# Two PSUM banks in one Relu instruction, and buffers that are cut by hand, in a fused attention and maxout kernel

## The chip, the core and the metric

The kernel runs on one core of a Trainium2 chip. The metric is the device time of one execution in microseconds (us); lower is better. The engines that appear below are TensorE (PE, matmuls; its weight loads are listed as PEld), VectorE (DVE), ScalarE (ACT), GpSimd (POOL) and SyncE (SP, which issues most DMAs). PSUM is the memory that PE writes its results to; it has 8 banks, and one bank holds 512 float32 numbers on each of 128 partitions.

## What is computed

Cut to what matters, with B = 4 batches of N = 12544 rows, C = 128 channels, 32 inducing points and J = 1024 hidden columns:

```python
def mab(q, kv):
    a = softmax(scale * q @ kv.T)
    return a @ kv
h = mab(inducing, x)              # 32 x 128 for each batch
y = mab(x, h)                     # 12544 x 128 for each batch
out = maximum(y @ w1, y @ w2) @ w_out
```

The kernel uses maximum(p, q) = p + relu(q - p). The part relu(y @ (w2 - w1)) @ w_out is the bulk of the work; y @ w1 @ w_out is one small matrix product, called the linear part.

## The kernel before

For each batch the rows are handled in chunks of 128 rows (98 chunks a batch). Up to 16 chunks make a block of four quarters, and a quarter holds up to four chunks. `stage` (L643) writes exp(scale * h x^T) of a block to SBUF, with the quarter q on the partitions 32q to 32q+31. Division by the sum of the exponentials is put off until the output.

A **phase** (L1031) takes up to four units, one for each quarter. A unit is 512 columns of hidden values: one to four matmuls with a contraction of 32 (L1085), which use only a quarter of PE's rows, so that four units run side by side. Each unit fills one PSUM bank. After the phase, each bank is **evicted**: Relu from PSUM to an SBUF tile in float16, by ACT (L1102) or DVE (L1105), whichever the planner thinks is free first. `final_one` (L920) then issues one full matmul (L932) that multiplies 128 hidden columns of a chunk by w_out and adds to the bank of the running **group** (a group is a quarter's chunks, up to four, in one bank that stays open for up to 32 such matmuls and a few of the linear part). `evict_group` (L954) divides by the sums, writes the result to SBUF and stores it with a DMA.

The order is written out by hand. `ORDER` (L1113) is a list of words: `p4.5` is a phase of four units whose bits in 5 swap the engine that the planner would choose, a number is that many final matmuls, `s` stages a block, `g3` transposes a block's exponentials with a DMA for POOL to sum, `x1.0` transposes x of the next batch, and so on. `Clock` (L21) is a planner: it adds up estimated durations to choose banks and engines while the program is built, and it is not run on the chip. All waits between engines are put in by the framework, which compares what each instruction reads and writes.

Before the steady part there is a ramp of some 27 us. Batch 0 of x is loaded by POOL's DMAs in twelve parts (`load_x`, L190, L195); each part is transposed (L276), multiplied by the inducing points (L292), put through exp (L305), and accumulated (L328) together with the sums of the exponentials (E sums, L319: up to four chunks of 32 columns by one matmul with a column of ones). Then come h, its product with w2 - w1 (`difference`, L572, and `small_hwd`, L506), and the weight work for the linear part: `cast_w1` (L576), `weights_2` (transposes, L589), `weights_2b` (L593) and `weights_3` (L603, eight matmuls at L607). `keep_busy` (L879) adds filler matmuls where the planner sees a gap.

PSUM tiles, Relu tiles and output tiles come from pools: a tile has a name of its own, and the framework knows which earlier tile held its place.

## Time and profile before

| what | value |
|---|---|
| median of 3 runs | 317.82 us (317.73 to 318.14) |
| profiled execution, its own time | 317.76 us |
| span of the profile (first to last instruction) | 316.0 us |
| PE busy | 308.6 us, 98% |
| ACT busy | 280.2 us, 89% |
| DVE busy | 274.5 us, 87% |
| POOL busy | 125.8 us, 40% |
| granted TensorE clock, mean | 0.998 |
| instructions | 12577 |

A busy share counts the time in which at least one instruction of the engine was running. In a group of instructions, the mean is of one instruction from its start to its end; since an engine starts the next one before the last has ended, a run of n takes less than n means. The chain of waits is followed back from the last instruction, and tells which engine's work set the end.

### The profile page before, as it was taken

Reading aid. Unit: us, or ns where it says so; the run is one execution under the profiler, and the core shown is the slowest. Engines: PE = TensorE matmul, PEld = TensorE weight load, DVE = VectorE, ACT = ScalarE, POOL = GpSimd, SP = SyncE. Lnnn points to the kernel's source line nnn. Section 1 sums busy time; section 2 is a strip of 40 time slices with the busy share of each in tenths; the row PEclk is TensorE's granted clock in tenths of the full one; section 3 lists DMA queues with packets and bytes.
Section 4 is the critical chain, followed back from the end, with each engine's and each line's share of the span. In section 5 each row is a group of like instructions: output and inputs, shape, how many; then the busy total and the mean of one; then the engine's idle time right before and its main releaser. Section 6 shows DMA issues by size and latency. Waiting matters only on the chain.

```text
span 316.0 us, 12577 instructions
## 1 busy us (share of the span) xinstructions
PE 308.6 (98%) x5308; PEld 239.9 (76%) x5308; DVE 274.5 (87%) x488; ACT 280.2 (89%) x580; POOL 125.8 (40%) x187
## 2 busy tenths in 40 slices
PE   6998999999999999999999999999999999999996
PEld 3885777777877777778877787887868777788885
DVE  2468999999878999988999899989899889999885
ACT  3669999999999999998999989899999999998891
POOL 7363060666620066067510064674406564461500
PEclk9999999999999999999999999999999999999999
DMA  8999999989799999898499999897323233324232
GB/s 203 208 252 205 207 219 146 207 229 230 127 218 245 245 183 174 190 233 207 121 225 252 213 227 215 204 174 203 106 85 118 100 106 118 119 88 140 102 120 101
DMA packets 81336, 55.81 MB, mean 177 GB/s; under 512 B 62816, under 2 KB 66176, under 8 KB 81280
## 3 DMA queue, kind: packets, MB, share of 16 engines
q1 hardware_dynamic: 75312, 41.32, 55.8%
q0 software_dynamic: 5968, 13.70, 22.4%
q8 instruction: 41, 0.67, 0.9%
q14 instruction: 15, 0.12, 0.1%
HBM read 27.28 MB, written 25.69 MB: 168 GB/s over the span
## 4 chain that ended last, share of the span: by engine, by line
PE 94%; DMA 2%; ACT 1%; DVE 1%; issue 1%; POOL 0%; POOLq 0%
PE ps L932 60%; PE ps L1085 23%; DMA xn<-in_x_dram 2%; PE ps L657 2%; PE ps L356 2%; PE ps L414 2%; PE ps L276 1%; PE ps L328 1%; PE ps L292 1%; PE ps L521 0%; DVE relu L1105 0%; PE ps L319 0%; ACT e L669 0%; DVE o L964 0%; ACT e_first L696 0%
## 5 line engine op out<-in xcount | busy, mean ns | idle before, releaser
L1102 ACT ACTIVATE relu<-ps 128x512 f16<-128x512 f32 x470 | 241.0, 627 | 17.5 <-PE ps L1085 16.5
L1105 DVE TENSOR_SCALAR relu<-ps 128x512 f16<-128x512 f32 x314 | 199.7, 684 | 20.6 <-PE ps L1085 19.0
L932 PE MATMUL ps<-woutp,relu 128*128 128x128 f16 x3136 | 203.5, 219 | 0.2
L932 PEld LDWEIGHTS <-relu 128*128 128x128 f16 x3136 | 176.6, 98 | 34.4 <-issue 28.7
L1085 PE MATMUL ps<-e,hwd 32*128 32x512 f16 (+2 forms) x840 | 82.8, 361 | 0.1
L720 POOL TENSOR_TENSOR half<-ed 128x256 f32<-128x256 f16 (+2 forms) x23 | 14.1, 613 | 145.8 <-DMA ed<-e 145.8
L724 POOL TENSOR_TENSOR rd<-den,minus 128x16 f32<-128x16 f32 (+2 forms) x23 | 60.7, 2639 | 1.8
L964 DVE TENSOR_TENSOR o<-ps,rd 128x512 f32<-128x512 f32 (+3 forms) x83 | 53.2, 643 | 3.9 <-PE ps L1085 2.8
L1085 PE MATMUL ps<-m,e 32*128 32x128 f16 x372 | 36.8, 216 | 0.0
L1085 PEld LDWEIGHTS <-hwd 32*128 32x128 f16 x880 | 26.7, 91 | 12.8 <-issue 3.8
L1085 PEld LDWEIGHTS <-e 32*128 32x128 f16 x372 | 22.4, 92 | 10.4 <-issue 2.7
L720 POOL TENSOR_TENSOR half<-half 128x32 f32<-128x32 f32 (+3 forms) x69 | 22.3, 323 | 5.4
L195 POOL DMA_DIRECT2D xn<-in_x_dram x32 | 17.6, 563 | 5.7 <-DMA xn<-in_x_dram 4.3
L280 DVE COPY xT<-ps 128x512 f16<-128x512 f16 (+3 forms) x12 | 5.7, 485 | 8.6 <-PE ps L276 8.6
L964 DVE TENSOR_TENSOR o<-ps,rp 128x512 f32<-128x512 f32 (+3 forms) x20 | 12.8, 642 | 0.0
L369 ACT ACTIVATE eu<-ps 128x512 f16<-128x512 f32 x18 | 11.0, 617 | 0.6 <-PE ps L356 0.3
L669 ACT ACTIVATE e<-ps 128x512 f16<-128x512 f32 (+2 forms) x21 | 11.1, 607 | 0.3 <-PE ps L657 0.2
L283 ACT COPY xT<-ps 128x768 f16<-128x768 f16 (+3 forms) x10 | 5.7, 574 | 4.3 <-PE ps L276 4.2
L276 PE MATMUL ps<-identity,xn 128*128 128x128 f16 x98 | 7.6, 220 | 1.4 <-DMA xn<-in_x_dram 0.9
L657 PE MATMUL ps<-xT,hT 128*32 128x512 f16 (+3 forms) x110 | 8.1, 361 | 0.1
L276 PEld LDWEIGHTS <-xn 128*128 128x128 f16 x98 | 5.5, 97 | 2.9 <-DMA xn<-in_x_dram 1.2
L356 PE MATMUL ps<-xT,inducingT 128*32 128x512 f16 x72 | 6.8, 386 | 0.0
(110 smaller groups left out, 117.7 us busy)
## 6 DMA issues: line engine op xcount, KB each, us to landing
out_dram<-o SPq DMA_DIRECT2D x90, 256.0 KB, 3.0
xn<-in_x_dram POOLq DMA_DIRECT2D x24, 448.0 KB, 10.4
out_dram<-o SPq DMA_DIRECT2D x10, 128.0 KB, 2.9
wf<-in_moe_w_dram POOLq DMA_DIRECT2D x4, 256.0 KB, 6.0
xn<-in_x_dram POOLq DMA_DIRECT2D x4, 224.0 KB, 10.2
xT<-xn SPq DMA_TRANSPOSE x33, 4.4
xf<-in_x_dram SPq DMA_DIRECT2D x1, 512.0 KB, 3.7
xf<-in_x_dram SPq DMA_DIRECT2D x1, 384.0 KB, 4.2
```

Of the source, the lines that this page charges most:

```text
L195: nc.gpsimd.dma_start(out=xn_at[b, i][:, 0:n, :], in_=xr[b, :, k0 : k0 + n, :])
L276: nc.tensor.transpose(ps[:, j, :], xn[:, g + j, :], identity16)
L356: nc.tensor.matmul(out=ps[32 * g : 32 * (g + 1), :], lhsT=inducingT, rhs=xT_tiles[b % 2][:, U * u + 4 * g : U * u + 4 * (g + 1), :], start ...
L657: nc.tensor.matmul(out=ps[32 * q : 32 * (q + 1), 128 * t : 128 * (t + n)], lhsT=hq, rhs=xT[:, c : c + n, :], start=True, stop=True, tile_p ...
L669: nc.scalar.activation(out=blk.e2[:, 0 : 128 * wd], in_=ps[:, 0 : 128 * wd], func=AF.Exp, scale=st[0]["rs"] if blk.b == 0 else scale,)
L720: nc.gpsimd.tensor_tensor(out=dst, in0=cur[:, :, 0:n], in1=cur[:, :, n : 2 * n], op=ALU.add)
L724: nc.gpsimd.tensor_tensor(out=rp[:, 0:wd, :].rearrange("p t q -> p (t q)"), in0=den[:, 0 : 4 * wd], in1=minus1[:, 0 : 4 * wd], op=ALU.pow,)
L932: nc.tensor.matmul(out=g.ps[:, 128 * c : 128 * (c + 1)], lhsT=g.blk.relu[g.q][:, 128 * (jb * w4 + t) : 128 * (jb * w4 + t + 1)], rhs=woutp ...
L964: nc.vector.tensor_mul(osb[:, 0:m, :], g.ps[:, 0 : m * C].rearrange("p (s c) -> p s c", s=m), g.blk.rp[:, t0 : t0 + m, q : q + 1].broadcas ...
L1085: nc.tensor.matmul(**seq.pop(0))
L1102: nc.scalar.activation(out=dst, in_=src, func=AF.Relu)
L1105: nc.vector.tensor_scalar(out=dst, in0=src, scalar1=0.0, scalar2=None, op0=ALU.max)
```

## The change

1. One persistent tensor `psall` [128, 8, 512] takes the place of the PSUM tiles; `bank()` gives slices of it. Four tensors `relus0` to `relus3` with two halves each, two small `relu1_` and one `osbs` with six slots take the place of the pools for Relu and output tiles.
2. `ORDER` has words with a third number (`p4.5.14`): its bits tell which quarters hold their unit back. The next phase of that quarter then evicts both banks with one instruction (`relu_out`, L1050 to L1076 of the new file), with 1024 columns from two banks, a step of b - a banks apart. `u` flushes what is held.
3. E sums take 4 and 3 (or 3 and 3) chunks instead of 4 and 2, and the last two parts of two chunks each share one matmul, so that none has 64 rows of output.
4. In the ramp, one half of `difference` and the second half of `cast_w1` go to POOL, `weights_2` is one step at a later place (`V`), and `weights_3` (`W`) comes later still. The loads of batch 1 are issued around them.
5. Part (0, 7) of x is loaded as 120 and 8 partitions. Seven small DMAs of 15 to 1 partitions copy a few values of part (0, 3) to an unused corner (`probe`).
6. `ORDER` and `EVICT` are new. Some of the planner's numbers are new.

```diff
-    relup = ctx.enter_context(tc.tile_pool(name="relup", bufs=2))
-    outp = ctx.enter_context(tc.tile_pool(name="outp", bufs=NOUT))
...
+    psall = psum.tile([128, 8, 512], F32, name="psall", tag="psall")
+    relus = [big.tile([128, 2, 4096], F16, name=f"relus{q}", tag=f"relus{q}") for q in range(4)]
+    relu1 = [big.tile([128, 1024], F16, name=f"relu1_{q}", tag=f"relu1_{q}") for q in range(2)]
+    osbs = big.tile([128, NOUT, 4, C], F32, name="osbs", tag="osbs")
...
-        uid[0] += 1
-        return i, psum.tile(shape, dtype, name=f"ps{uid[0]}", tag=f"bank{i}", bufs=1)
+        ps = psall[:, i, :]
...
+        return i, ps
...
-        nc.gpsimd.dma_start(out=xn_at[b, i][:, 0:n, :], in_=xr[b, :, k0 : k0 + n, :])
+        cuts = (0, 120, 128) if (b, i) == (0, 7) else (0, 128)
+        for lo, hi in zip(cuts, cuts[1:]):
+            nc.gpsimd.dma_start(out=xn_at[b, i][lo:hi, 0:n, :], in_=xr[b, lo:hi, k0 : k0 + n, :])
...
+        for i, k in enumerate((15, 14, 12, 8, 4, 2, 1)):
+            nc.sync.dma_start(out=probe[0:k, 16 * i : 16 * i + 8 + i], in_=xn_at[0, 3][0:k, 0, 0 : 8 + i])
...
+        SUMS = {
+            14: ((0, 4), (4, 4), (8, 3), (11, 3)),
+            7: ((0, 4), (4, 3)),
+            6: ((0, 3), (3, 3)),
+            4: ((0, 4),),
+        }
+        pair16 = head16[:, 1024 : 1024 + 4 * M].rearrange("p (k m) -> p k m", m=M)
...
-                for j in range(lo, hi, 4):
-                    m = min(4, hi - j)
+                if n > 2:
+                    cuts = [(et, j, m) for j, m in SUMS[n]]
+                else:
+                    cuts = [(pair16, 0, 4)] if last else []
+                for src, j, m in cuts:
...
-                nc.scalar.copy(out=w1h[:, sl], in_=w1f[:, sl])
-                w_of["cast", h] = ck.on_act(21.7, 0.45)
+                nc.gpsimd.tensor_copy(out=w1h[:, sl], in_=w1f[:, sl])
+                w_of["cast"] = ck.on_pool(0.0, 0.8)
...
-        for i in range(7):
-            if i == 3:
-                difference(nc.gpsimd, 512, J, 22.4, 1.2)
+        load_x(1, 0)
+        difference(nc.vector, 0, 256, 21.0, 0.34)
+        difference(nc.gpsimd, 256, 512, 21.0, 0.64)
+        load_x(1, 1)
+        load_x(1, 2)
+        difference(nc.gpsimd, 512, J, 22.9, 1.25)
+        cast_w1(1)
+        for i in range(3, 7):
             load_x(1, i)
-        difference(nc.vector, 0, 256, 21.0, 0.3)
         sums = small_h(0)
-        difference(nc.vector, 256, 512, 21.0, 0.3)
-        weights_2(0)
...
-            blk.relu[q] = relup.tile([128, 1024 if small else 4096], F16, name=f"relu_{uid[0]}", tag=tag, bufs=bufs)
+            blk.relu[q] = relu1[q % 2] if small else relus[q][:, len(past) % 2, :]
...
-            osb = outp.tile([128, 4, C], F32, name=f"o_{uid[0]}", tag="o")
+            osb = osbs[:, g.index % NOUT, :, :]
...
+        def relu_out(qs, units, banks, ready, flip):
+
+            q, blk = qs
+            _, t0, w, u = units[0]
+            n, jpb, w4 = len(units), 4 // w, blk.quarters[q].w
+            src = psall[:, banks[0], :]
+            dst = blk.relu[q][:, 0 : NJB * w4 * 128].rearrange("p (j t) -> p j t", j=NJB)
+            dst = dst[:, u * jpb : (u + n) * jpb, 128 * t0 : 128 * (t0 + w)]
+            if n == 2:
+                a, b = banks
+                src = psall[:, a : (b + 1 if b > a else b - 1 if b else None) : b - a, :]
+                src = src.rearrange("p v (j t) -> p v j t", j=jpb)
+                dst = dst.rearrange("p (v j) t -> p v j t", v=2)
+            else:
+                src = src.rearrange("p (j t) -> p j t", j=jpb)
+            on_act, on_dve = ((0.477, 0.597), (0.904, 1.13))[n - 1]
+            if (max(ck.act, ready) + on_act <= max(ck.dve, ready) + on_dve) != flip:
+                nc.scalar.activation(out=dst, in_=src, func=AF.Relu)
+                t = ck.on_act(ready, on_act)
+            else:
+                nc.vector.tensor_scalar(out=dst, in0=src, scalar1=0.0, scalar2=None, op0=ALU.max)
+                t = ck.on_dve(ready, on_dve)
...
-        def phase(n, flip=0):
+        def phase(n, flip=0, hold=0):
...
+                nxt = (blk.units[q] + [None])[blk.units[q].index(unit) + 1]
+                if q in holds:
+                    _, first, b0, _ = holds.pop(q)
+                    relu_out((q, blk), [first, unit], [b0, bi], ready, bool(flip >> k & 1))
+                elif hold >> k & 1 and nxt and nxt[1:3] == unit[1:3] and nxt[3] == unit[3] + 1:
+                    holds[q] = (blk, unit, bi, ready)
+                    ck.bank[bi] = INF
+                else:
+                    relu_out((q, blk), [unit], [bi], ready, bool(flip >> k & 1))
...
-        s p4.13 s H1 W g2 p4.1 p2 8 m0 4 p3 p2.1 10 p3 p2 13 p3.2 6 p4.5 22 p2 p4.8 17 x1.0 p4.8 4 g1 11
...
+        p4.5.14 p1.1 u s s s H1 V g2 4 p4.4.9 p2 u W 4 p3.2 s 4 m0 8 p2 p3.1 4 x1.0 4 x1.1 8 p2 p3.2 10
...
+            "V": weights_2,
...
+            "u": flush,
```

More of the change, by code (lines that the diff above doesn't have):

```diff
@@ L170 @@
     uid = [0]
+    psall = psum.tile([128, 8, 512], F32, name="psall", tag="psall")
+    relus = [big.tile([128, 2, 4096], F16, name=f"relus{q}", tag=f"relus{q}") for q in range(4)]
+    relu1 = [big.tile([128, 1024], F16, name=f"relu1_{q}", tag=f"relu1_{q}") for q in range(2)]
+    osbs = big.tile([128, NOUT, 4, C], F32, name="osbs", tag="osbs")
     def bank(shape, dtype=F32, only=None):
         i = min(range(8), key=lambda j: ck.bank[j]) if only is None else only
-        uid[0] += 1
-        return i, psum.tile(shape, dtype, name=f"ps{uid[0]}", tag=f"bank{i}", bufs=1)
+        ps = psall[:, i, :]
+        if dtype == F16:
+            ps = ps.bitcast(F16)
+            if len(shape) == 3:
+                ps = ps.rearrange("p (k c) -> p k c", c=128)
+            ps = ps[:, 0 : shape[1]]
+        return i, ps
     NXN = 12
@@ L213 @@
     identity16 = consts.tile([128, 128], F16, name="identity16")
-    head16 = relup.tile([128, 4096], F16, name="head", tag="relu3")
+    head16 = relus[3][:, 0, :]
     head = head16.bitcast(F32)
@@ L223 @@
     minus1 = consts.tile([128, 16], F32, name="minus1")
-    wf = relup.tile([128, 4096], F16, name="wf", tag="relu0").bitcast(F32)
+    wf = relus[0][:, 0, :].bitcast(F32)
     w1f, w2f = wf[:, 0:J], wf[:, J : 2 * J]
-    w1s = relup.tile([128, 4096], F16, name="w1s", tag="relu1")
+    w1s = relus[1][:, 0, :]
     w1h = w1s[:, 0:J]
@@ L235 @@
     repd = consts.tile([128, 128], F32, name="repd")
+    probe = relus[2][0:16, 1, 3968:4096]
     pace = consts.tile([128, 1], F32, name="pace")
     with tc.manual_schedule(engines={ET.PE, ET.DVE, ET.Activation, ET.Pool, ET.SP}):
-        xf = relup.tile([128, 4096], F16, name="xf", tag="relu2")[:, 0 : 256 * P1].bitcast(F32)
+        xf = relus[2][:, 0, 0 : 256 * P1].bitcast(F32)
         xf = xf.rearrange("p (k c) -> p k c", c=C)
@@ L264 @@
         st = [dict() for _ in range(B)]
-        LANDED = [0.0, 7.58, 9.72, 11.95, 13.05, 14.12, 16.27, 17.37, 18.31, 18.94, 19.26, 19.57]
+        LANDED = [0.0, 7.58, 9.72, 11.95, 13.03, 14.1, 16.3, 17.37, 18.28, 18.95, 19.33, 19.66]
         def p1_transpose(b, i, half):
@@ L302, in p1_scores @@
             else:
-                at = 1024 + 2 * M * (i % 2)
-                et = head16[:, at : at + 2 * M].rearrange("p (k m) -> p k m", m=M)
+                et = pair16[:, 2 * (i % 2) : 2 * (i % 2) + 2, :]
             nc.scalar.activation(out=et[:, 0:n, :], in_=ps[:, 0 : n * M], func=AF.Exp, scale=scale)
@@ L316, in p1_accum @@
                 ck.wait(ready, "p1")
-                for j in range(lo, hi, 4):
-                    m = min(4, hi - j)
+                if n > 2:
[3 more added lines that the diff above has]
+                for src, j, m in cuts:
                     nc.tensor.matmul(
                         out=st[0]["eps"][0 : m * M, 0:1],
-                        lhsT=et[:, j : j + m, :].rearrange("p k m -> p (k m)"),
+                        lhsT=src[:, j : j + m, :].rearrange("p k m -> p (k m)"),
                         rhs=ones16[:, 0:1],
                         start=(i == 0 and j == 0),
-                        stop=(last and j + m == n),
+                        stop=last,
                         skip_group_check=True,
@@ L334, in p1_accum @@
                     )
-                st[0]["end"] = ck.run(0.0285 * (hi - lo) + 0.015 * ((hi - lo + 3) // 4))
+                st[0]["end"] = ck.run(0.026 * (hi - lo) + 0.022 * len(cuts))
                 return
@@ L371, in pool_scores @@
             )
-            ck.bank[bi] = ck.on_act(end, 0.65)
+            ck.bank[bi] = ck.on_act(end, 0.575)
             st[b]["eu", u] = eu, ck.bank[bi]
@@ L544, in small_hwd @@
                     st[b]["hw", piece] = ck.bank[bi]
-        def second_half(vector):
-            small_hwd(0, (2,), bool(vector))
-            weights_2(1)
-            weights_2b(1)
         def small_m1(b):
@@ L579, in cast_w1, with weights_2 @@
                 nc.vector.tensor_copy(out=w1h[:, sl], in_=w1f[:, sl])
-                w_of["cast", h] = ck.on_dve(20.4, 0.33)
+                ck.on_dve(20.4, 0.33)
             else:
-                nc.scalar.copy(out=w1h[:, sl], in_=w1f[:, sl])
-                w_of["cast", h] = ck.on_act(21.7, 0.45)
-        def weights_2(g):
-            bi, ps = bank([128, 4, 128], F16)
-            for j in range(4):
-                jb = 4 * g + j
-                nc.tensor.transpose(ps[:, j, :], w1h[:, 128 * jb : 128 * (jb + 1)], identity16)
-            w_of["ps", g] = ps, bi, ck.run(0.056 * 4, ready=max(ck.bank[bi], w_of["cast", g]), why="w")
-            ck.bank[bi] = INF
-        def weights_2b(g):
-            ps, bi, end = w_of["ps", g]
-            if g == 0:
-                nc.vector.tensor_copy(out=w1T[:, 0:4, :], in_=ps)
-                ck.bank[bi] = w_of["w1T"] = ck.on_dve(end, 0.34)
-            else:
-                nc.scalar.copy(out=w1T[:, 4:8, :], in_=ps)
-                ck.bank[bi] = w_of["w1T"] = max(w_of["w1T"], ck.on_act(end, 0.48))
+                nc.gpsimd.tensor_copy(out=w1h[:, sl], in_=w1f[:, sl])
+                w_of["cast"] = ck.on_pool(0.0, 0.8)
+        def weights_2():
+            turned = []
+            for g in range(2):
+                bi, ps = bank([128, 4, 128], F16)
+                for j in range(4):
+                    jb = 4 * g + j
+                    nc.tensor.transpose(ps[:, j, :], w1h[:, 128 * jb : 128 * (jb + 1)], identity16)
+                turned.append((bi, ps, ck.run(0.056 * 4, ready=max(ck.bank[bi], w_of["cast"] if g else 0.0), why="w")))
+                ck.bank[bi] = INF
+            for g, (bi, ps, end) in enumerate(turned):
+                if g == 0:
+                    nc.vector.tensor_copy(out=w1T[:, 0:4, :], in_=ps)
+                    ck.bank[bi] = w_of["w1T"] = ck.on_dve(end, 0.34)
+                else:
+                    nc.scalar.copy(out=w1T[:, 4:8, :], in_=ps)
+                    ck.bank[bi] = ck.on_act(end, 0.48)
+                    w_of["w1T"] = max(w_of["w1T"], ck.bank[bi])
         def weights_3():
@@ L672, in stage @@
             )
-            blk.staged = ck.bank[bi] = ck.on_act(end, 0.05 + wd * 128 / 1200.0)
+            blk.staged = ck.bank[bi] = ck.on_act(end, (0.143 if blk.b == 0 else 0.05) + wd * 128 / 1200.0)
         def stage_first(blk):
@@ L698, in stage_first @@
                 )
-                blk.staged = ck.bank[bi] = ck.on_act(max(end, st[0]["rsr"]), 0.05 + 256 / 1200.0)
+                blk.staged = ck.bank[bi] = ck.on_act(max(end, st[0]["rsr"]), 0.143 + 256 / 1200.0)
                 if h == 0:
@@ L744, in relu_slot @@
             past.append((blk, q))
-            uid[0] += 1
-            blk.relu[q] = relup.tile([128, 1024 if small else 4096], F16, name=f"relu_{uid[0]}", tag=tag, bufs=bufs)
+            blk.relu[q] = relu1[q % 2] if small else relus[q][:, len(past) % 2, :]
             return blk.relu[q]
@@ L843 @@
         ck.on_dve(0.0, 0.07)
-        cast_w1(1)
-        weights_2b(0)
         groups, ends = [], [0] * 4
@@ L901 @@
         held = []
+        holds = {}
         def linear_full():
@@ L955, in evict_group @@
             n = len(g.chunks)
-            uid[0] += 1
-            osb = outp.tile([128, 4, C], F32, name=f"o_{uid[0]}", tag="o")
+            osb = osbs[:, g.index % NOUT, :, :]
             q, t0 = g.chunks[0]
@@ L1003, in next_job @@
             unit = blk.units[q][u]
+            if ("hw", ((unit[3] + 1) * (4 // unit[2]) - 1) // 2) not in st[blk.b]:
+                return None
             if relu_slot(blk, q) is None:
@@ L1029, in pick, with flush @@
             return gl, [e[1:] for e in sorted(jobs, key=lambda e: e[1])]
-        def phase(n, flip=0):
+        def relu_out(qs, units, banks, ready, flip):
[19 more added lines that the diff above has]
+                t = ck.on_dve(ready, on_dve)
+            for bi in banks:
+                ck.bank[bi] = t
+            for _, t0, _, u in units:
+                blk.done[q, t0, u] = t
+        def flush():
+            for q in sorted(holds):
+                blk, unit, bi, ready = holds.pop(q)
+                relu_out((q, blk), [unit], [bi], ready, False)
+        def phase(n, flip=0, hold=0):
             gl, jobs = pick(n)
@@ L1093, in phase @@
                     evict_group(gl, end)
-            for k, (q, blk, (_, t0, w, u), bi, ps, _) in enumerate(got):
-                jpb = 4 // w
-                w4 = blk.quarters[q].w
-                dst = blk.relu[q][:, 0 : NJB * w4 * 128].rearrange("p (j t) -> p j t", j=NJB)
-                dst = dst[:, u * jpb : (u + 1) * jpb, 128 * t0 : 128 * (t0 + w)]
-                src = ps.rearrange("p (j t) -> p j t", j=jpb)
-                ready = ends[k] + 0.03
-                if (max(ck.act, ready) + 0.477 <= max(ck.dve, ready) + 0.597) != bool(flip >> k & 1):
-                    nc.scalar.activation(out=dst, in_=src, func=AF.Relu)
-                    t = ck.on_act(ready, 0.477)
-                else:
-                    nc.vector.tensor_scalar(out=dst, in0=src, scalar1=0.0, scalar2=None, op0=ALU.max)
-                    t = ck.on_dve(ready, 0.597)
-                ck.bank[bi] = t
-                blk.done[q, t0, u] = t
+            for k, (q, blk, unit, bi, _, _) in enumerate(got):
+                ready = ends[k] + 0.03
@@ L1109, in phase @@
                 ptr[q][1] += 1
                 state["issued"] += 1
+                nxt = (blk.units[q] + [None])[blk.units[q].index(unit) + 1]
[4 more added lines that the diff above has]
+                    holds[q] = (blk, unit, bi, ready)
+                    ck.bank[bi] = INF
+                else:
+                    relu_out((q, blk), [unit], [bi], ready, bool(flip >> k & 1))
@@ L1112 @@
         state["stage"] = 1
         ORDER = """
-        s p4.13 s H1 W g2 p4.1 p2 8 m0 4 p3 p2.1 10 p3 p2 13 p3.2 6 p4.5 22 p2 p4.8 17 x1.0 p4.8 4 g1 11
-        p4.1 13 p4.9 p1 16 p3.4 p2 14 p4.10 6 x1.1 4 x1.2 x1.3 x1.4 x1.5 x1.6 2 p3.6 s s s s 6 g3 6 p4.5
-        14 x1.7 1 x1.8 p4.8 19 p4.10 p2.1 12 x1.9 5 p3 14 p4.4 c1.0 15 p1 p4.5 14 p4.3 g4 13 p4.8 25 p4.6
-        p3.2 10 x1.10 17 p2 p3.1 15 c1.1 p4.2 12 t1.1 2 p3 6 p4.2 4 g5 11 c1.2 c1.3 p4.1 18 p4.4 t1.3 21
-        p3.5 p3 22 c1.4 p1.1 p4.1 19 p2 p4.8 5 g6 21 p4.2 p2 c1.5 19 r1 a1.1 p3.2 p4 t1.5 19 a1.3 p4.9
@@ L1119 @@
-        p2.2 29 p3.3 p4 26 p4.1 a1.5 5 p3.1 p2.3 1 e1 11 p4.12 1 h1 17 w1 s s s s p3.2 19 m1 15 p4.6 p3.6
-        30 p3.1 p3.3 24 p3 p3.3 27 p3.2 p3.1 20 p4.3 p2 15 s p4.1 18 p2.1 p3 15 g7 g8 7 p3.3 p4.2 9 g9 12
-        x2.0 3 x2.1 x2.2 s p1.1 p4.4 x2.3 12 p4.5 14 p4.6 14 p4 14 p3 21 p3.6 p4.8 14 g10 4 x2.4 4 x2.5
-        x2.6 9 p4.13 s c2.0 14 p4.6 p1 5 x2.7 4 x2.8 13 p3.3 p3.4 23 p4.4 11 c2.1 p4 p1 9 t2.1 4 g11 x2.9
-        4 x2.10 10 p4.3 p3 15 c2.2 p3.3 21 p3.1 p3.5 27 p3.3 p3.2 c2.3 19 p4.10 4 g12 4 t2.3 5 p4.1 17
@@ L1124 @@
-        p3.1 p3.4 16 a2.1 c2.4 p3.1 p3.1 23 p4.4 18 p2.1 p4.9 13 g13 17 p4.9 p3.3 24 a2.3 c2.5 p4.1 p2 7
-        t2.5 12 r2 18 p3 p4.2 30 p4.10 p2.2 16 a2.5 p4.3 p3.6 8 e2 10 p4.2 2 h2 21 p3.1 p3.6 11 w2 4 m2
-        15 p4.11 s s s 13 p3 p2 12 s p4 15 p2 p3.2 22 p3.5 p3.2 3 x3.0 4 x3.1 19 p3.4 p4.12 25 p3.3 13 p3
-        p3.3 27 p3.2 p3.5 12 g15 8 g14 3 p4 11 s s p3.1 p2.2 14 x3.2 4 x3.3 4 x3.4 x3.5 5 p3.1 p4.5 19
-        x3.6 17 p3.4 p4.1 23 g16 14 p4.4 p3 27 c3.0 s p3.1 15 x3.7 c3.1 p4.2 p1 x3.8 15 p4.4 21 p3.4 p3 8
@@ L1129 @@
-        g17 14 p3.3 p2 6 t3.1 12 p4.2 p1 20 p3.4 p3.4 22 p4.10 p2.1 30 p4.3 p3 4 g18 8 x3.9 4 x3.10 7
-        c3.2 a3.1 c3.3 p4.3 p2 9 t3.3 15 p4.4 17 p2.1 p4.8 27 p2.2 p4.1 13 g19 18 p3.3 p4.4 10 r3 8 c3.4
-        c3.5 a3.3 p4.5 20 t3.5 1 p4.8 p2.2 21 p4.4 13 p3.5 p2 1 g20 27 p4.4 p3.3 27 a3.5 p4.8 p2.3 2 e3
-        16 h3 14 p3.5 p4.2 10 w3 4 m3 15 s p4.1 9 g21 10 p3.1 p2.1 15 p3.5 s s s 13 p3.1 p3.4 22 p4.8 p1
-        27 p4.3 p3 9 g22 13 p2.2 p2 22 p3.2 p4.3 25 s s p3.4 13 p3 p3.3 30 p4.9 p3.2 g23 21 p4.2 20 p4.1
@@ L1134 @@
-        p2.2 30 p3.4 p4.2 24 s p2 p3.2 12 p4.8 g24 22 p4.6 p2.2 20 p2.1 p3.2 16 p3.1 p2 11 p4.9 21 p4.3 9
-        p1 p3 g25 p1 20 p3.1 p3.4 30 p4.8 p3.1 26 p4.8 13 p4.6 13 p4.3 9 g26 13 p3.3 p3 27 p3.5 p2 22 p2
-        p4.1 22 p2.2 p4.9 22 p3 p2.1 g27 27 p4.1 p3.2 38 p4.3 p3.1 31 p2 p4.9 22 p2.1 p3.1 24 p3 p4.11 40
-        p3.4 p3 21 p4.6 21 p2.1 p3.4 31 p4.4 p4.3 63
+        p4.5.14 p1.1 u s s s H1 V g2 4 p4.4.9 p2 u W 4 p3.2 s 4 m0 8 p2 p3.1 4 x1.0 4 x1.1 8 p2 p3.2 10
+        p4.3 19 p2.2.2 p4 11 g3 8 g1 p4 10 p4.2 14 p4.5.1 p1.1 u 4 x1.2 x1.3 4 x1.4 x1.5 4 x1.6 x1.7 4
@@ new lines @@
+        p3.3.1 p2.1 u 14 p4.3 s s 6 x1.8 6 p3.5 9 p4.4 5 g4 12 p4.10 17 p4.2.4 p2 28 p3.5.4 p4.5 22 c1.0
+        p1.1.1 p4.1 12 p4.2 13 g5 1 p4.6 25 p4.9.9 p3.2 10 x1.9 4 x1.10 10 c1.1 p2.0.1 p3.1 12 p4 6 t1.1
+        22 p3.2.2 p4 18 g6 5 c1.2 c1.3 p4.1 15 p4.3 22 p3.0.7 p3 u t1.3 27 p1 p4.5 14 p2.0.1 p3.1 5 r1 19
+        p4.0.6 p2.2 u 13 a1.1 c1.4 p3.2 c1.5 9 p4.6 a1.3 t1.5 7 p4.13.13 p2.1 30 p3.1.1 p4.4 27 p4.9 a1.5
+        5 p3.2.4 p2.3 u 2 e1 11 p4.11 1 h1 17 w1 s s s s p3.1 3 m1 31 p4.5.6 p3.6 u 29 p3.0.4 p3.3 22
@@ new lines @@
+        p3.0.2 p3 26 p3.3 p4.4 21 p3.2.4 p2.2 u 15 s p4 20 p2.1.3 p3 u 16 g7 g8 7 p3.2.2 p4.1 9 g9 12
+        x2.0 4 x2.1 x2.2 s p1 p4.2 x2.3 x2.4 x2.5 13 p4 14 p4.6 14 p4.1 12 p3 22 p3.1.3 p4.10 13 g10 15
+        p4 16 c2.0 s p4.13.7 p1.1 u 5 x2.6 4 x2.7 4 x2.8 9 c2.1 p3.0.4 p3 7 t2.1 14 p4.2 13 p4.2.5 p1 u
+        13 g11 x2.9 4 x2.10 11 p4.5.10 p3 u 22 c2.2 p3.2 13 p3.2 p3.4 27 p3.0.2 p3.3 u c2.3 19 p4.4 4 g12
+        4 t2.3 4 p4.4 18 p3.1 p3.3 17 a2.1 c2.4 p3.2.2 p3 21 p4.9 4 r2 16 p2.0.3 p4.7 12 g13 18 p4.5.8
@@ new lines @@
+        p3.6 24 a2.3 c2.5 p4.13.10 p2 6 t2.5 28 p3.0.2 p4.5 29 p4.13.15 p2 u 19 a2.5 p4.0.10 p3.1 8 e2 10
+        p4.4 2 h2 21 p3.3.3 p3.6 u 11 w2 4 m2 14 p4.7 s s s 13 p3.5 p2 15 s p4.4 11 p2.0.2 p3.2 23 p3.1.1
+        p3 4 x3.0 4 x3.1 18 p3.0.6 p4.2 26 p3 11 p3.1.2 p3.5 27 p3.2 p3.2 14 g15 3 p4.8 5 g14 11 s s
+        p3.7.7 p2.3 u 17 x3.2 4 x3.3 4 x3.4 x3.5 3 x3.6 p3.3.5 p4.6 37 p3.6.2 p4.4 24 g16 14 p4.8.3 p3.4
+        23 p3 11 p4.6.3 p1 u 8 x3.7 4 x3.8 6 s c3.0 c3.1 p4.5 21 p3.4.4 p3.6 u 13 g17 9 p3.4.7 p2.2 u 11
@@ new lines @@
+        t3.1 13 p4.11.9 p1 u 19 p3.4 p3.4 25 p4.6.5 p2.2 u 29 p4.10.10 p3.2 u g18 10 x3.9 4 x3.10 8 c3.2
+        a3.1 c3.3 p4.4.9 p2 u 8 t3.3 15 p4.4 18 p2.3.1 p4.1 26 p2.0.1 p4.1 9 g19 22 p3.2.2 p4 10 r3 8
+        c3.4 c3.5 a3.3 p4.1 16 t3.5 5 p4.4 p2.2 22 p4.9 10 p3.3.2 p2.1 g20 29 p4.2 p3.3 27 a3.5 p4.0.1
+        p2.1 3 e3 24 h3 6 p3.2 p4.13 10 w3 8 m3 12 s p4.2 12 g21 4 p3.5.4 p2.2 u 16 p3.5 s s s 16 p3.3.1
+        p3.4 21 p4.8.9 p1 u 27 p4.9.4 p3 12 g22 10 p2.0.1 p2 21 p3.1.4 p4.2 25 s s p3.2 14 p3.4.5 p3 29
@@ L1138 @@
+        p4.3.3 p3.2 u 1 g23 24 p4.6 17 p4.14.4 p2.1 u 31 p3.1 p4.2 25 s p2.1 p3.2 11 p4.3 g24 22 p4.6.6
+        p2 u 21 p2.1 p3.1 12 p3.1 11 p2.1.1 p4.9 23 p4.2 10 p1 p3.1 g25 p1 19 p3.1.2 p3.1 29 p4.3 p3 21
+        p4.5 14 p4.1 14 p4.2 16 g26 5 p3.1 p3.2 27 p3.2 p2 20 p2.2 p4.5 23 p2.2.3 p4.6 28 p4.0.9 p2.2 u 1
+        g27 28 p4.6.6 p3.1 37 p4.8.10 p3.2 30 p2 p4.6 23 p2.3 p3.1 28 p3.0.5 p4.2 42 p3.6.4 p3.3 u 18
+        p3.2 21 p3.0.7 p3.3 27 p4 p4 62
         """
-        EVICT = "000000000000000000000000101000000000000000000000010000000000000000000010000000000000000000000000000000010000"
+        EVICT = "000000000000000000000000101000000000000000000000010000000000000000000010000000000000000000000000001000101000"
@@ L1152 @@
             "g": lambda k: turn_e2(blocks[k]),
-            "H": second_half,
+            "H": lambda v: small_hwd(0, (2,), bool(v)),
+            "V": weights_2,
             "W": weights_3,
             "f": linear_full,
+            "u": flush,
             "p": phase,
```

## The prediction

> **What bounds the kernel now.** I read the page's busy shares and its chain of waits first, then the groups by shape, then a timeline of one stretch in the steady part, and last the ramp.

> ```profile
> PE 308.6 (98%) x5308; PEld 239.9 (76%) x5308; DVE 274.5 (87%) x488; ACT 280.2 (89%) x580; POOL 125.8 (40%) x187
> ...
> PE 94%; DMA 2%; ACT 1%; DVE 1%; issue 1%; POOL 0%; POOLq 0%
> ```

> PE's own work sets the end: 94% of the chain. ACT and DVE are nearly full, yet hardly ever on the chain. So a cheaper eviction gives nothing by itself; it only counts where PE waits. By the starts of the matmuls in the trace, 2814 of 2966 steps between neighbouring final matmuls are under 60 ns, and a change of tile shape costs about 0.11 us. Beyond these, after 27 us, PE loses 4.7 us in 45 small waits. That is all that a better order can win there.

> ```profile
> L1102 ACT ACTIVATE relu<-ps 128x512 f16<-128x512 f32 x470 | 241.0, 627 | 17.5 <-PE ps L1085 16.5
> L1105 DVE TENSOR_SCALAR relu<-ps 128x512 f16<-128x512 f32 x314 | 199.7, 684 | 20.6 <-PE ps L1085 19.0 <-ACT relu L1102 0.6
> ...
> L1085 PE MATMUL ps<-e,hwd 32*128 32x512 f16 x712 | 82.0, 381 | 0.1
> ...
> L283 ACT COPY xT<-ps 128x768 f16<-128x768 f16 x4 | 3.2, 798 | 2.5 <-PE ps L276 2.5
> ...
> L964 DVE TENSOR_TENSOR o<-ps,rd 128x256 f32<-128x256 f32 x6 | 2.5, 420 | 1.4 <-PE ps L1085 1.1 <-PE ps L909 0.3
> ...
> L283 ACT COPY xT<-ps 128x384 f16<-128x384 f16 x4 | 1.9, 478 | 1.7 <-PE ps L276 1.7
> ```

> These are the prices: one eviction lasts 0.63 (ACT) or 0.68 us (DVE). A pair of 1024 columns isn't shown. From above it is two singles (1.25, 1.37), from below one (0.63, 0.68). By the slope of ACT's copies, (798 - 478)/384 = 0.83 ns a column, it is 627 + 427 = 1.05 us; by DVE's 683 (L964, 512 columns) and 420 (256), 1.03 ns a column, 1.21 us. I take these.

> Now one stretch: phases up to 114.6, then finals.

> ```profile
> 114.06 0.39 PE L1085 MATMUL ps<-e,hwd 32*128 32x512 f16 x3
> ...
> 114.29 0.38 PE L1085 MATMUL ps<-e,hwd 32*128 32x512 f16 x4
> 114.48 2.56 ACT L1102 ACTIVATE relu<-ps 128x512 f16<-128x512 f32 x5 [0.43 <-PE ps L1085]
> ...
> 114.60 1.90 PE L932 MATMUL ps<-woutp,relu 128*128 128x128 f16 x31
> 114.74 1.29 DVE L1105 TENSOR_SCALAR relu<-ps 128x512 f16<-128x512 f32 x2 [0.54 <-PE ps L1085]
> ```

> This is the picture that the kernel lives on. The finals start at 114.60 in the open group's bank, while DVE evicts the phases' other banks until 116.03 and ACT until 117.04. Over the 66 stretches of phases that run straight into finals, their last eviction ends 1.28 us after the first final starts (middle 90%: 0.81 to 1.77). Finals hide evictions.

> **The change, part by part.**

> *Pairs.* By the changed program's list of instructions, 128 of the 784 units leave in 64 pairs: 48 on ACT, 16 on DVE. That saves 48 x (1.25 - 1.05) + 16 x (1.37 - 1.21) = 12 us of overlapping records, in back-to-back time some 0.05 us each, 3 us: nothing on PE's path. But PSUM is now one tensor, and the list also names the waits. Of the 64 pairs only 10 take neighbouring banks; 54 step over others. The framework treats such a pair as if it read every bank from the lower to the higher. An example from the list, banks in brackets:

> ```
> ACT  relu_out  evicts [3]
> ACT  relu_out  evicts [5] and [0]      waits for PE
> PE   final_one adds to [2]             waits for that ACT pair
> ```

> Bank 2 is the group's: its last true reader is long done. Still the first final waits for the pair, and everything on PE stands behind it. The same rule makes pairs wait for the other engine's evictions of banks in between (55 waits of ACT for DVE, 43 of DVE for ACT, some long met). The list has 34 waits of PE for an eviction that touches none of the banks concerned; at 25 the waiting matmul is a final right behind the phase, with the pair just sent off.

> The price of one, from rows and without a backlog: in the example, ACT can begin 0.38 (L1085) + 0.07 (its shortest start after a matmul) = 0.45 us into the stretch, the single takes 0.49 (the run of seven singles in 3.54 us at 26.86 gives (3.54 - 0.63)/6), the pair 1.05, a wait some 0.05: PE goes on at 2.04. Without the wait finals start at 0.43 (two rounds of 0.216) + 0.11 = 0.54. Stall 1.5 us. With two singles ahead of the pair it is 2.0. The worst place has a DVE pair [0, 5] behind ACT's [4, 7] and [1]: 0.45 + 0.91 + 0.61 + 1.21 + 0.05 - 0.54 = 2.7. At the 25 places I see chains of these lengths; I take 1.9 on average, 25 x 1.9 = 47.5 us. Bounds: 1.3 (the mean lag above, which now is waited for in full) and 2.5 (a backlog on most). PE's idle time doesn't come back: its work stays the same. The other nine waits have mostly over 1 us of PE work ahead of them: 2 us in all (0 to 4).

> [...]

> *PE's own work.* The list has as many phase, final and stage matmuls as before. Runs of one tile shape go from 354 to 336; 14 of the 18 belong to the E sums. Four changes fewer at 0.11, one phase round of 0.22 more: -0.2 us. The 4.7 us of small waits: planned anew, and partly swallowed by the stalls, since ACT and DVE catch up in them. I take -3 (0 to -4.7).

> *Ramp.* (a) E sums: a 64-row sum and what follows take 90 + 120 ns from start to start where others take 25 + 25. Three of seven stand behind the last load, at 20.4 to 21.5, on the path to h: -0.5 us. The other four are hidden by loads. (b) `weights_3` waits for ACT's copy:

> ```profile
> PE ps L607 <- ACT w1s L599: 1.0, 1, 1.0
> ```

> With W later this goes: -1.1 us with the gap around it (0 if something else is late at that place; next is the eviction of the first phases). Two filler matmuls (L891) go: -0.2. (c) Part (0, 7) in two: from part (0, 6) on, one of the sixteen shares of each load lands 1 us after the others (16.36 against 15.20), because a 16 KB instruction fetch at 14.22 held one DMA engine for 0.98 us. If that share is rows 120 to 127, the last x lands up to 0.9 us sooner. PE idles only 0.7 us between 16.5 and 20.5, so I take -0.3 (+0.1 to -0.6). (d) Moved to POOL: half a `difference` (half of L573's 1.27) and a cast (0.54 to 1.27, the nearest rows: L262 memset and L573, both 512 columns). They delay the last four loads of batch 1 by up to 1.9 us. The load before these occupies the DMA until 31.7, 7 us after they were issued: hidden; without that cover the first transposes of batch 1 (SP, 36.5) would be late. POOL's extra issue of 0.55 us falls into its 5.7 us of waiting for loads. The seven probe DMAs stand on SP between 12 and 25.6, where it has nothing else: at 0.4 us each 2.8 us, hidden. Sum of the ramp -2.1 (0 to -2.8).

> *Output evictions, persistent outputs.* Six more of 0.38 us on ACT late in the kernel, beside PE: 0. The six output slots and two halves per Relu tensor are as many as before: 0.

> **Sum.** Against the profiled execution's 317.76 (span 316.0, median of the runs 317.82, so the sum stands for the median too): 317.8 - 2.1 - 0.2 - 3 + 47.5 + 2 = **362 us**. Lowest with all ends: 317.8 - 2.8 - 0.2 - 4.7 + 32.5 = 343; highest 317.8 + 0 - 0.2 - 1 + 62.5 + 4 = 383.

> **Rivals.**

> *Faster, 312.5 us.* The in-between waits are met by the time that PE comes to them, and ramp and order give their 5.3 us. This decides below 5.3/25 = 0.2 us a stall. For it: evictions can start 0.07 us after a matmul. Against: even the earliest last eviction in the trace ends 0.8 us after the first final. 7%. That the difference falls within 0.2% (what a measurement of this kernel can tell from no change): 2%.

> *Short stalls, about 328 us.* PE's waiting empties ACT's and DVE's queues, and only some 0.6 us is left of each: 317.8 - 5.3 + 15 = 327.5. For it: today's median start of an ACT eviction is 0.59 us late, all backlog. Against: the sums above have none. 10%.

> *The clock falls, about 393 us.* Rows first: the nine warm-up matmuls of 512 columns start 0.43 us apart, later ones 0.22; the 1.1 us gap at L607 left the granted clock at 1.00 in the windows 21 to 26 and 26 to 32. If 25 gaps of 2 us put a tenth of PE's work (31 us) at half rate, 362 + 31 = 393. 5%. [...]

> *Forecast:* 76%. Range 327 to 385: the forecast's own span with most of the short stalls; outside are faster, same and the clock, and the ends of the others. Faster 7%, same 2%, slower 91%.

> **What would show it.** PE's busy share falls to about 86%; the waits get a line with some 25 entries of "PE ps (the finals) waiting for ACT relu", longest near 2.5 us, 40 us or more with DVE's; ACT and DVE fall below 80% with about 280 and 275 us or less of busy time. L607's wait is gone, and PE's first final comes about 1 to 2 us sooner. If the finals' waits are few or short, the price of a stall was wrong; if they are missing, the reading of the list was.

## The result, and the profile after

The changed kernel takes 387.88 us (median of four runs, 385.45 to 392.40) against 317.77 us before. The ratio is 1.218, 95% interval 1.210 to 1.226. The forecast was 362 us with a range of 327 to 385, so the direction and the stalls came out and the size did not. The profiled execution of the changed kernel is the slowest of the four (392.40 us, mean granted clock 0.948; the other three, over which the ratio is taken, had 0.960 to 0.972), so the sums below are made for that one, against the 316.0 us span of before.

The page after: the span, busy time of each engine, the granted clock in 40 slices, and the shares of the chain.

```profile
span 390.6 us, 12548 instructions
...
PE 329.1 (84%) x5305; PEld 253.2 (65%) x5305; DVE 274.1 (70%) x465; ACT 285.1 (73%) x541; POOL 128.0 (33%) x190
...
PEclk9999958888999999989999989978988999999999
...
PE 64%; ACT 13%; DVE 7%; issue 3%; ACTq 0%; DVEq 0%
```

PE is busy 84% of the span and no longer carries the chain alone: evictions hold a fifth of it. ACT and DVE have about as much work as before (280.2 and 274.5 us then) and more time. Two things are to be seen: PE waits, and its clock, 9 throughout before, has dips.

PE's waits after: the instruction, whom it waited for, us in total, times, the longest.

```profile
PE psall L950 <- ACT relus L1067: 36.5, 21, 2.7
PE psall L950 <- DVE relus L1070: 14.2, 7, 3.0
PE psall L1137 <- ACT relus L1067: 2.2, 4, 1.0
PE psall L1137 <- DVE relus L1070: 1.3, 2, 0.7
```

The view of before has no line of this kind. L950 is the final matmul: 28 times it stood behind an eviction, for 50.7 us. One such place, from the timeline (start, length, engine, what; in brackets the idle time before it and who ended it):

```profile
169.35 0.38 PE L1137 MATMUL psall<-e,hwd 32*128 32x512 f16 x3
169.88 2.06 ACT L1067 ACTIVATE relus<-psall 128x512 f16<-128x512 f32 x4 [0.71 <-PE psall L1137]
171.49 1.22 DVE L1070 TENSOR_SCALAR relus<-psall 128x1024 f16<-128x1024 f32 x1 [1.79 <-ACT relus L1067]
172.77 0.44 PE L950 MATMUL psall<-woutp,relus 128*128 128x128 f16 x5 [3.04 <-DVE relus L1070]
```

In the program the DVE pair reads banks 7 and 4, ACT's singles read 1, 2, 5 and 3, and the group's bank is 6. The pair counts as a reader of 4 to 7, so DVE waits 1.79 us for ACT's eviction of bank 5, and the final, which adds to bank 6, waits 3.04 us for the pair. Neither shares a bank with what it waits for. Before, such a final started 0.31 us after the start of the phase's last round (114.29 and 114.60 in the stretch shown ahead of the result).

What that does to the clock, in stretches of the same place (from:to, length, busy time with instructions, granted clock, DMA share, GB/s):

```profile
160.00:170.00 10.00, 9.73 (x182) 1.00 1.14 232
170.10:172.70 2.60, 0.00 (x0) 1.00 0.05 18
172.80:173.50 0.70, 0.70 (x14) 1.00 0.00 0
173.60:177.00 3.40, 3.40 (x37) 0.51 0.26 87
```

PE stands idle for 3.04 us at full clock (the second row is the inner part of that), works 0.9 us at full clock, and then runs for 3.41 us at half of it.

I split PE's lost time in the profiled executions by the starts of neighbouring matmuls, less what the same step takes elsewhere in the trace (56 ns for 128 columns, 0.216 us for a round of 512, 0.11 us for a change of tile shape):

| part | before | after |
|---|---|---|
| waits for a pair that touches none of the waiting instruction's banks | 0 | 56.4 us in 32 places |
| extra time of matmuls at half clock | 0 | 16.5 us in 12 windows of 3.41 us |
| other waits over 0.06 us | 11.6 us | 15.3 us |
| PE's needed work at full clock | 296.9 us | 295.3 us |

56.4 + 16.5 + 3.7 - 1.6 = 75.0 us; the spans differ by 74.6.

### The profile page after: what moved, and what is told of

Read it like the earlier page. It is cut to its first block, busy times and chain, and to the rows that moved or that the text cites. A ratio compares the mean times of both kernels' runs of the same rounds, so it can differ in the third digit from the quotient of the medians.

```text
span 390.6 us, 12548 instructions
## 1 busy us (share of the span) xinstructions
PE 329.1 (84%) x5305; PEld 253.2 (65%) x5305; DVE 274.1 (70%) x465; ACT 285.1 (73%) x541; POOL 128.0 (33%) x190
## 4 chain that ended last, share of the span: by engine, by line
PE 64%; ACT 13%; DVE 7%; issue 3%; ACTq 0%; DVEq 0%
PE psall L950 44%; PE psall L1137 16%; ACT relus L1067 12%; DVE relus L1070 6%; PE psall L378 2%; PE psall L436 1%; PE psall L675 1%; DVE osbs L981 1%; ACT e L687 0%; PE psall L543 0%; ACT eu L391 0%; PE psall L481 0%; PE psall L927 0%; ACTq L1067 0%; DVE hacc L469 0%
## 5 line engine op out<-in xcount | busy, mean ns | idle before, releaser
L1067 ACT ACTIVATE relus<-psall 128x512 f16<-128x512 f32 (+1 forms) x421 | 242.0, 658 | 74.1 <-PE psall L1137 62.9
L950 PE MATMUL psall<-woutp,relus 128*128 128x128 f16 x3104 | 212.9, 226 | 50.1 <-ACT relus L1067 36.5
L950 PEld LDWEIGHTS <-relus 128*128 128x128 f16 x3104 | 186.5, 101 | 85.1 <-issue 79.8
L1070 DVE TENSOR_SCALAR relus<-psall 128x512 f16<-128x512 f32 (+1 forms) x291 | 195.5, 713 | 64.5 <-PE psall L1137 39.8
L1137 PE MATMUL psall<-e,hwd 32*128 32x512 f16 (+2 forms) x840 | 88.0, 376 | 4.2 <-ACT relus L1067 2.2
L981 DVE TENSOR_TENSOR osbs<-psall,rd 128x512 f32<-128x512 f32 (+3 forms) x81 | 52.4, 647 | 25.7 <-PE psall L950 15.8
L1137 PE MATMUL psall<-m,e 32*128 32x128 f16 x372 | 39.6, 223 | 0.0
L391 ACT ACTIVATE eu<-psall 128x512 f16<-128x512 f32 x18 | 10.8, 604 | 14.0 <-PE psall L378 13.7
L981 DVE TENSOR_TENSOR osbs<-psall,rp 128x512 f32<-128x512 f32 (+3 forms) x20 | 12.9, 643 | 5.8 <-issue 2.3
L687 ACT ACTIVATE e<-psall 128x512 f16<-128x512 f32 (+2 forms) x21 | 11.1, 603 | 1.3 <-PE psall L675 1.2
```

The source lines that it names most:

```text
L391: nc.scalar.activation(out=eu, in_=ps, func=AF.Exp, scale=scale, accum_out=st[b]["es"][:, u : u + 1])
L687: nc.scalar.activation(out=blk.e2[:, 0 : 128 * wd], in_=ps[:, 0 : 128 * wd], func=AF.Exp, scale=st[0]["rs"] if blk.b == 0 else scale,)
L950: nc.tensor.matmul(out=g.ps[:, 128 * c : 128 * (c + 1)], lhsT=g.blk.relu[g.q][:, 128 * (jb * w4 + t) : 128 * (jb * w4 + t + 1)], rhs=woutp ...
L981: nc.vector.tensor_mul(osb[:, 0:m, :], g.ps[:, 0 : m * C].rearrange("p (s c) -> p s c", s=m), g.blk.rp[:, t0 : t0 + m, q : q + 1].broadcas ...
L1067: nc.scalar.activation(out=dst, in_=src, func=AF.Relu)
L1070: nc.vector.tensor_scalar(out=dst, in0=src, scalar1=0.0, scalar2=None, op0=ALU.max)
```

## The experiments

**Theory.** A pair over two banks is treated as a reader of all the banks between them; the false waits that follow cost some 56 us, and the long ones among them cost 16 us more through the clock. **Rivals:** pairs as such cost the time (a bank is held longer, ACT and DVE wait for each other); the new order, the persistent tensors or the ramp do; the clock is lost for a reason of its own.

All variants of the changed kernel replace the pair's instruction in `relu_out` by this (shortened), with a condition of their own for `split`; the planner's accounts, and so list, engines and banks, stay as they are unless it is said:

```
-                nc.scalar.activation(out=dst, in_=src, func=AF.Relu)
+                for d, s in both:      # both = [(dst, src)], or, where split,
+                    nc.scalar.activation(out=d, in_=s, func=AF.Relu)
+                                       # [(dst[:, v], src[:, v]) for v in range(2)]
```

(and the same for DVE). Results, each with its ratio to the kernel before, run beside it:

| kernel | pairs | median us | ratio, 95% interval |
|---|---|---|---|
| changed | 64 | 387.88 | 1.218 (1.210 to 1.226) |
| singles only | 0 | 317.87 | 1.0008 (0.998 to 1.0035) |
| pairs clear of group banks | 42 | 333.71 | 1.048 (1.045 to 1.052) |
| the 11 long ones | 11 | 355.10 | 1.114 (1.110 to 1.119) |
| the 23 short ones | 23 | 345.90 | 1.087 (1.084 to 1.091) |
| neighbouring pairs as they fall | 19 | 317.94 | 0.9998 (0.9985 to 1.0010) |
| neighbouring banks, up to 0.3 us late | 24 | 318.31 | 1.0010 (0.9996 to 1.0024) |
| neighbouring banks, up to 2 us late | 52 | 332.53 | 1.045 (1.043 to 1.047) |
| no unit held | 0 | 330.08 | 1.038 (1.036 to 1.040) |
| singles, no cut, no probes | 0 | 317.86 | 1.0001 (0.9987 to 1.0014) |
| singles, old E sums | 0 | 318.53 | 1.0016 (1.0003 to 1.0028) |
| before, new E sums | 0 | 317.76 | 0.9997 (0.9985 to 1.0010) |

**Singles only** (`split` always).

> The changed kernel with each of its 64 pairs sent as two instructions of one bank each, one behind the other on the same engine and at the same place of the list; all else as changed. False waits (a pair over banks a and b is treated as a read of all the banks between them): the 34 waits of PE and the half-clock windows behind them go, 387.9 - 56 - 16 = 316 us, 312 to 319. Order, persistent tensors or ramp at fault: the loss stays with the list, 350 us or more. Clock lost for another cause: the stalls go, the half-clock windows stay, about 332 us.

317.87 us: the whole loss goes with the pairs. Order, tensors and ramp are not at fault, and the clock is not lost for another reason. The page's busy times, clock and chain:

```profile
PE 308.9 (98%) x5305; PEld 240.3 (76%) x5305; DVE 271.8 (86%) x481; ACT 283.7 (90%) x589; POOL 127.8 (40%) x190
...
PEclk9999999999999999999999999999999999999999
...
PE 93%; DMA 3%; DVE 2%; issue 1%; POOL 0%; ACT 0%; POOLq 0%; DVEq 0%
```

**Pairs clear of group banks.** `split = any(min(banks) < x < max(banks) for x in open_banks())`, the banks of open and held groups.

> Pairs kept, except where the bank of an open or held output group lies strictly between the two banks (22 of 64): those go as two singles. 42 pairs stay, and 12 of the 34 false waits of PE, which cost 10.8 us in the changed kernel's trace. False waits: the time with singles only plus 11 us and little of the clock's loss, 322 to 334 us. Pairs as such at fault (a bank held longer, ACT and DVE waiting for each other): two thirds of the loss of 70 us stays, about 362 us.

333.71 us, 15.8 more than singles. Its trace has 10.7 us of false waits, one half-clock window that cost 1.5 us, and 4.6 us more of other waits. Two thirds of the pairs are there and less than a quarter of the loss: what counts is what lies between the banks.

**Long and short stalls.** `split` by the pair's number in the program: all but 11, or all but 23.

> Only the 11 pairs kept whose final waited 2.1 us or longer in the changed kernel's trace (28.1 us in all); the other 53 as two singles. If long stalls bring the half-clock windows: singles + 28 us + some 6 windows of 3.41 us, each of which costs 1.2 to 1.7 us of PE's work: singles + 36 us, 352 us, PEclk with several digits below 9. If the clock falls for another cause: singles + 28, 344 us, and as many windows as with the short ones.

> Only the 23 pairs kept whose PE instruction waited 0 to 1.94 us in the changed kernel's trace (28.3 us in all, about the sum of the 11 long ones); the other 41 as two singles. If long stalls bring the half-clock windows: singles + 28 us and at most two windows, 344 to 347 us, PEclk nearly all 9. If the clock falls with the waiting in sum, whatever its pieces: as much as with the long ones, about 352 us.

The two have nearly the same waiting, 27.6 us in 11 places and 27.3 us in 21, and differ by 9.2 us. Page and PE's waits of the long ones, then of the short ones:

```profile
PEclk9989997888999999998999999998999999999999
...
PE psall L950 <- ACT relus L1073: 13.8, 6, 2.7
PE psall L950 <- DVE relus L1077: 12.9, 5, 2.8
```

```profile
PEclk9999999999999999999999999999999999999999
...
PE psall L950 <- ACT relus L1073: 22.6, 15, 1.9
PE psall L950 <- DVE relus L1077: 0.7, 1, 0.7
```

Seven half-clock windows (one of them in the ramp) cost 9.9 us in the first; the second has none before the last 0.5 us of its span. 315.7 (span of singles) + 27.3 + 0.6 of other waits = 343.6 against a span of 343.4; with the long ones 315.7 + 27.6 + 9.9 + 0.5 = 353.7 against 353.4. The granted clock of all four runs of each says the same: 0.961 to 0.976 with the long stalls, 0.994 to 0.999 with the short ones. So the clock is lost to long stalls, not to waiting in sum. The long ones came 3 us above what I expected, 2 of them because I had put singles at 316 us.

**Neighbouring pairs as they fall.** `split = abs(banks[0] - banks[1]) > 1`.

> The changed kernel with its own banks and list; only the 19 pairs whose banks are neighbours stay pairs (12 on ACT, 7 on DVE), the other 45 go as two singles. Nothing of the planner's choices changes. False waits alone at fault: 317.9 us, within 0.3 us of singles only. Pairs as such at fault: 19/64 of the 70 us, 338 us. Cheaper evictions a gain: 317.4 us or less.

317.94 us. A pair whose range holds nothing else costs nothing, and gains nothing.

**Neighbouring banks chosen.** In `phase`, for the second unit of a pair (cut):

```
+                if q in holds:
+                    near = [j for j in free if abs(j - holds[q][2]) == 1 and ck.bank[j] <= ck.bank[bi] + 2.0]
+                    bi = near[0] if near else bi
```

with 2.0 in one kernel and 0.3 in the other; `split` as for neighbouring pairs.

> Pairs only of neighbouring banks, and the second unit of a pair gets the bank beside the first one's if that comes free at most 2 us later by the planner's clock; other pairs go as two singles. 52 pairs stay, 38 on ACT and 14 on DVE, and no PE instruction waits for an eviction that touches none of its banks. False waits alone at fault: 317 to 321 us (the time with singles only, 317.9, and up to 3 us of true waits for a bank chosen late), PEclk 9 throughout. Pairs as such at fault (a bank held longer, ACT and DVE waiting for each other): 52/64 of the 70 us, about 375 us.

> As the kernel with 52 neighbouring pairs, but the neighbouring bank is taken only if it comes free at most 0.3 us later: 24 pairs, 18 on ACT and 6 on DVE, no false wait of PE besides the two that singles have. False waits alone at fault: 317 to 318.5 us, within 0.3% of singles only, since an eviction cheaper by some 0.1 us shortens nothing that PE waits for. If cheaper evictions do count: 24 x 0.2 us over two engines, some 2 us less, 315.5 us. Pairs as such at fault: 24/64 of 70 us, 344 us.

The second came as expected. The first missed: 332.53 us, 12 more than the upper end, though far from the 375 us of pairs as such. Its waits say why:

```profile
PE psall L1149 <- ACT relus L1073: 4.1, 8, 0.7
PE psall L1149 <- DVE relus L1077: 2.4, 4, 0.6
...
PE psall L1149 <- DVE osbs L981: 1.1, 2, 0.7
...
PE psall L1149 <- ACT osbs L988: 0.6, 1, 0.6
```

Now phases (L1149) wait; none of these lines is in singles only, the finals stand free but once (0.3 us), the clock is full, and other waits are 26.8 us against 12.7. The twelve waits of the first two lines all end with an eviction of 512 columns, one bank, and none with a pair. That fits banks that were chosen late, and I had taken those to be worth 3 us in all. But the planner's other engines and banks changed with them, and the same banks were not run with singles, so what the 14 us are made of is argued, not shown.

**No unit held.** Each unit evicted behind its own phase: `elif hold >> k & 1 and ...` becomes `elif False`.

> Singles only, and each unit is evicted behind its own phase instead of waiting for its partner (the planner's choice of engine and bank follows from that; the words of the list are the same). The singles-only kernel starts its first final 1.8 us sooner than before and ends at the same time, 317.9 us. If held units cause the small waits that eat the lead: 316.3 to 317.3 us. If the list or the ramp's later waits do: 317.5 to 318.5 us.

330.08 us, outside both: no false wait, full clock, but other waits of 24.7 us against 12.7, spread over some thirty phases at up to 0.59 us. The list's engine bits and counts were written for held units, and with another choice of engines and banks they probably no longer fit; no run tests that. So this run leaves open what a hold costs.

**The ramp's parts**, each on singles only: without cut and probes (`cuts = (0, 128)`, the seven DMAs left out), and with the old E sums (`cuts = [(et, j, min(4, n - j)) for j in range(0, n, 4)]`); then the new E sums alone in the kernel before.

> Singles only, without the load cut in two and without the seven small probe transfers on SP; all else as changed. If cut and probes bring the late load share forward as forecast, this is 0.3 us slower than singles only, 318.2 us; if not, as the traces say (the last load lands 0.35 us sooner in the changed kernel, one share stays about 1 us behind the others), within 0.2 us of 317.9.

> Singles only, with the kernel before's E sums (groups of four from each part and a 64-row group at the end of five parts and for each of the two last ones). If the sums without 64 rows shorten the path to h by 0.5 us, as forecast, and the lead lasts: 318.4 us. If what follows in the ramp swallows it (the weight differences on POOL and the load that they wait for): within 0.2 us of 317.9, with the last accumulation 0.4 to 0.5 us later and the first phase by less.

> The kernel before with one part of the change alone, the E sums without 64 rows (no pairs, tensors, list and planner's clock as before). If the sums shorten the path to h by 0.5 us and the lead lasts to the end: 317.4 us, a ratio of 0.9985. If weights_3's wait for ACT's copy, which stays in this kernel, swallows the lead: 317.8 to 318.0 us.

Cut and probes: no difference (the profiled execution of that kernel, 319.25 us, has a half-clock window in its ramp at 17.1, which may be why it lies 1.4 us above the median). E sums: without them 0.6 us more than the neighbouring pairs measured beside them, with intervals that overlap. In the kernel before they gain nothing that can be told: the wait of `weights_3` for ACT's copy, which in the changed kernel is gone, is still there and no shorter (PE's waits of that kernel):

```profile
PE ps L617 <- ACT w1s L609: 1.1, 1, 1.1
```

No version beat both kernels by more than its interval.

## Why the prediction was right and wrong, by its own steps

- **The mechanism: right.** The in-between rule, read from the list of instructions, was the whole loss: without the pairs the ratio is 1.0008, with pairs over nothing 0.9998. One count was wrong: 19 of the 64 pairs take neighbouring banks, not 10 (the others go downwards, from bank b+1 to b). No term used it.
- **Price of a pair: right.** 1.05 and 1.21 us were estimated, 1.027 and 1.221 measured. ACT's busy time did not fall with it: about 280 us or less was expected, 285.1 came. The groups by shape after (instruction, count, busy time, mean ns, idle before):

```profile
L1067 ACT ACTIVATE relus<-psall 128x1024 f16<-128x1024 f32 x48 | 49.0, 1027 | 10.7 <-DVE relus L1070 8.1 <-PE psall L1137 2.4
...
L1070 DVE TENSOR_SCALAR relus<-psall 128x1024 f16<-128x1024 f32 x16 | 19.5, 1221 | 9.4 <-ACT relus L1067 7.7 <-PE psall L1137 1.6
```

  The second half of each line is the cross-wait of ACT and DVE, 15.8 us, which the chains of the prediction held.
- **25 finals x 1.9 us = 47.5: right.** The trace has 26 of 0.9 us or more with 51.9 us, a mean of 2.0. The place that was called the worst was put at 2.7 and took 2.9; the longest stall of all, the one shown above, took 3.0 at another place. The rivals of short stalls and of waits already met fall. PE's share (86% forecast, 84% seen), ACT's and DVE's below 80%, and the first final 1.55 us sooner (25.53 against 27.08) came as the prediction's last part asks.
- **Nine other waits, 2 us: too small.** Beside those 26 finals, six places cost 4.5 us, and two of the 34 waits cost nothing.
- **Ramp -2.1, PE's own work -0.2, small waits -3: did not come as time.** Singles only, which has all of them, stands within some 0.3 us of before. The E sums gave about what was forecast (0.5 forecast, 0.6 measured with wide ends), `weights_3`'s wait went, and the first phase came at 22.55 instead of 23.44. Then other waits took the place of the one removed, at the same spot, by singles' timeline:

```profile
24.35 0.38 PE L543 MATMUL psall<-w,hT 128*128 128x512 f16 x1 [0.27 <-POOL w L590]
...
25.98 0.72 PE L1144 MATMUL psall<-e_first,hwd 32*128 32x128 f16 x13 [0.34 <-DVE hwd L547]
```

  The weight difference on POOL (L590) itself waits 0.27 us for a load. By 100 us singles have 1.6 us less needed work (most of it E sums) and 0.5 us more lost time, a lead of 1.0; from 100 to 310 us they lose 3.6 us to waits and small steps and the kernel before 2.8, so that 0.2 us is left. The new list has no fewer small waits (5.6 us after 27 us, 5.1 before, counted alike): "-3" had no row behind it, only the room that there was. (The highest sum also took 1 us off for them where its stated end was 0; with 0 it is 384 instead of 383, which changes nothing.)
- **The clock: the step that failed.** It stood as a rival of 5%, priced at 31 us, and the sum had no term for it. The reason given was that the one gap of 1.1 us in the trace left the clock at 1.00. But my own forecast had gaps of 1.9 us on average and up to 2.7, and no row of that trace showed a gap between matmuls above 1.1; a gap half as long was no evidence. What it cost was 16.5 us in the profiled execution, 1.0 to 1.6 us a window. The four runs had spans of 383.7, 384.5, 387.7 and 390.6 us at mean granted clocks of 0.972, 0.968, 0.960 and 0.948. If the clock that each lost is priced as in the profiled one, an estimate, its part is 8.7, 9.9, 12.5 and 16.5 us, and without it all four spans lie between 374 and 375.2 us. So the clock also accounts for the spread of the runs, and without it the median too would lie within the range, near 377 us.

From 362 to the profiled 392.4: clock +16.5, gains that did not come +5, finals +4.4, other false waits +2.5, which makes 390.4; for the 2.0 that are left, the changed kernel has 2.6 us more of other waits than singles. Less the clock's part, 375.9 us, this time would lie within the range.

The runs bear the rival of a falling clock out for stalls of about 2 us and more (27.6 us in the 11 places of the long-stall kernel: seven half-clock windows, the one in the ramp among them, 9.9 us), and not for the 21 shorter ones of the short-stall kernel (27.3 us, no such window before the last 0.5 us).

## What to carry to other kernels

Cutting buffers by hand from one tensor gives the dependency tracker ranges instead of names: an access with a stride over banks then waits for, and holds back, everything in between (here 56.4 us in 32 waits of PE), so look at the waits of the built program and give such pairs neighbouring banks, or none. Price a stall of TensorE twice, once as idle time and once through the clock (here 56.4 and 16.5 us), and do not take a short gap of the old trace for evidence on a longer one that the change brings. Cheaper evictions on engines that hardly ever end the chain (DVE 2% of it, ACT 0% in singles only) gained nothing here: 19 harmless pairs moved the time by less than 0.15%.
